# Attention and a token and channel mixer on one core: far tiles in one transfer, the ring of weight tiles on SyncE, and sums of weights stored at once

## The chip, the cores and the metric

The kernel runs on one core of a Trainium2 chip. The metric is the device time of one execution in microseconds. A core has TensorE (PE in the profile; PEld are its weight loads), VectorE (DVE), ScalarE (ACT), GpSimd (POOL) and SyncE (SP). DMAs are issued here by SyncE and by ScalarE, in the order of their programs, and run on 16 DMA engines.

## What is computed

The reference, cut to what matters (batch 8, 8 heads, 576 positions, head size 64, all float32):

```python
# attention inside chunks of 64 positions
scores = (q_c @ k_c^T) / sqrt(64)            # (8, 8, 9, 64, 64)
attn = softmax(scores)                       # with + 1e-9 in the denominator
x = (attn @ v_c) as (8, 576, 512)            # heads side by side
# mixer
h  = relu(x^T @ w_tok1) @ w_tok2             # over positions: 576 -> 256 -> 576
u  = x + h^T
h2 = relu(u @ w_ch1) @ w_ch2                 # over channels: 512 -> 1536 -> 512
return u + h2
```

## The kernel before, in words

Every float32 operand of the mixer is split into two float32r parts, high and low, and a product is three matmuls (high by high, low by high, high by low). The 4608 columns (batch by position) are handled in stages.

*First batch* (to about 210 us): the weights are converted, split and kept in SBUF while the first 576 columns go through both mixers.

*Single blocks* (to about 350 us): two blocks of 512 columns. Each runs 12 steps of a first channel matmul `ch1` and 12 of a second, `ch2`; a counter `now` (0 to 47) counts them, one step being 12 matmuls of 512 columns. Beside them run *bursts* of attention for the later batches (`attention`, called from a list of steps), and the preparation of Strassen-Winograd products: `sum_step` adds and splits blocks of the weights, 24 halves in all, each into one buffer of tag `sparts` (`SUM_BUFS` = 3); those of `c1` are made on GpSimd, those of `c2` on VectorE, at the steps in `SUMS`. The third step of a half puts its two blocks on the list `dumps`, where blocks of the raw weights (`dump_raw`, three at each step of `RAW_AT`) stand too; `dump(DUMPS)` stores two of the list to DRAM in each step, in order, from SyncE (L872).

*Pairs* (from about 350 us): three pairs of blocks run as products of that scheme, 84 per pair: 42 of the first channel weights (`product`, L1064) and 42 of the second (L1244), six matmuls each. Product k reads half of a *ring* tile, 512 KB, which comes back from DRAM. Ring tiles (`RING` = 5) are asked for by `load_product`, on ScalarE's queue, in ScalarE's order (`in_turn` holds an instruction behind the last one of its engine): the load of tile t stands at product 2t - 7, and its buffer is free after product 2t - 9. The function `unit(s)` is called behind product s and runs bursts (nine in pair 0, four in pair 1, every 7 or 8 products), loads and the mixing of the next pair. At s = 40 and 44 the token weights are read back (`load_tokens`), needed from s = 66.

*A burst* k scores tile k, and multiplies the probabilities of tile k - 2 with v in one PSUM tile. VectorE subtracts the maximum, ScalarE takes the exponential, `far_out` transposes 32 by 32 blocks on VectorE (L387) and SyncE writes them to DRAM (L392); `far_in` reads them back transposed, in four DMAs, one for each 32 partitions (L398): into `pf` for the probabilities (issued one step, or in the pairs four products, behind the burst; copied to `pt` ahead of burst k + 2), and into `xt` for the output x, which also goes to `xh` and `xl` for the token mixer.

The order of SyncE's instructions is that of the program in all stages. TensorE's is written out by hand from the end of the first batch; the others follow a planner's estimate of time, except what stands in `in_turn`. The framework gives the DMAs of both queues one of eight completion semaphores in turn; an issue waits on its own queue until the transfer that had that semaphore before has landed.

Of the kernel before, what the change touches and what calls it, by code (L numbers as in the profile page):

```python
# [18 lines left out]
P = 128  # L19
# [27 lines left out]
KH = 2 * P  # L47
RING = 5
LAG = 2
# [50 lines left out]
def attention_mixer_kernel(ctx, tc, qk_in, vo_in, v_in, w1_in, w2_in, wc1_in, wc2_in, out):  # L100
# [192 lines left out]

    def load_qk(i):
        qk = pool.tile([P, 2, NHP, P], F32, tag="qk" if i > 4 else "qk0", name="qk", bufs=3 if i > 4 else 5)
        nc.sync.dma_start(out=qk.rearrange("p a b c -> p (a b c)"), in_=qk_in[i])
        tiles[i] = {"qk": qk}

    def load_v(i):
# [7 lines left out]
        nc.sync.dma_start(out=v.rearrange("p a b c -> p (a b c)"), in_=src)  # L307
        tiles[i]["v"] = v

    def attn_load(i):  # L310
        load_qk(i)
        load_v(i)
# [550 lines left out]
    wide = ctx.enter_context(tc.tile_pool(name="wide", bufs=1, space=bass.MemoryType.DRAM))  # L863
    stored, tokens, dumps = {}, {}, []

    def dump(n):

        for key, src in dumps[:n]:
            two, one = divmod(products.index(key), 2)
            if two not in stored:  # L870
                stored[two] = wide.tile([P, 2, 2, KH], F32, tag=f"w_{two}", name="w")
            nc.sync.dma_start(out=stored[two][:, one], in_=src if src.dtype == F32 else src.bitcast(F32))  # L872
        del dumps[:n]
# [7 lines left out]
    def store_token():  # L881

        keys = [p[0] for p in plan[:token]] + ["half"]
        if len(tokens) < len(keys):
            key = keys[len(tokens)]
            src = half_all[0] if key == "half" else tops[key, "parts"]
            d = wide.tile([P, 2, src.shape[-1]], F32, tag="wt_" + "_".join(map(str, key)), name="wt")
            nc.sync.dma_start(out=d, in_=src.bitcast(F32))
            tokens[key] = d
# [32 lines left out]
    def attention(k):  # L922
# [3 lines left out]
        attn_both(i, j)  # L926
        if k + 2 < len(order):
            attn_load(order[k + 2])
        load_waiting(1)
        if i is not None:  # L930
            attn_p(i)
            tiles[i]["far"] = far_out(tiles[i]["pr"])
            attn_z(i)
        ready = len(waiting)
        if j is not None:
# [60 lines left out]
    def sum_step(kind, p, step):  # L996
# [40 lines left out]
        else:  # L1037
            for k, n in enumerate(SUM_KEYS[kind][half]):
                dumps.append(((kind, p, n), of[half][:, k]))

    def dump_raw(p):

        for n, f, h in ((0, 2 * p, 0), (3, 2 * p + 1, 1), (5, 2 * p + 1, 0)):
            dumps.append((("c2", p, n), weights["c2", f][:, :, h * KH:(h + 1) * KH]))

    ring = []
    def load_product(upto):
        while len(ring) < min(upto, PAIRS * len(products)):
            w = pool.tile([P, 2, 2, KH], F32, tag="ring", name="ring", bufs=RING)
            with in_turn():  # L1050
                nc.scalar.dma_start(out=w, in_=stored[len(ring) % len(products) // 2])
            ring.extend(w[:, one] for one in range(2))

    def product(i, u, width):

        load_product(i + 2 * RING - 2)
        if i % 3:
# [4 lines left out]
        for j in range(2):  # L1062
            for q, (wi, ui) in enumerate(THREE):
                nc.tensor.matmul(  # L1064
                    ps, lhsT=w[:, wi, j * P:(j + 1) * P].bitcast(F32R), rhs=u[ui][j],
                    start=j == 0 and q == 0, stop=j == 1 and q == 2,
                )
        return ps

    def load_tokens(kinds):  # L1070

        for key, d in tokens.items():
            if (key if key == "half" else key[0]) not in kinds:
                continue
            w = pool.tile(list(d.shape), F32, tag="again_" + "_".join(map(str, key)), name="again", bufs=1)
# [60 lines left out]
    def pair(n, rs):  # L1136
# [10 lines left out]
        def unit(s):  # L1147
# [31 lines left out]
        for p in range(NFC // 2):  # L1179
# [50 lines left out]
        for s, (step, p) in enumerate(steps):  # L1230
            while len(ready) <= min(s + SPLIT_AHEAD, len(steps) - 1):
                ready.append(operand(*steps[len(ready)]))
            load_product(first + PRODUCTS + s + 2 * RING - 2)
            if s == 0:
# [7 lines left out]
            for m in range(2):  # L1242
                for q, (wi, gi) in enumerate(THREE):
                    nc.tensor.matmul(  # L1244
                        accs[m], lhsT=w[:, wi, m * P:(m + 1) * P].bitcast(F32R), rhs=ready[s][gi],
                        start=p == 0 and q == 0 and step in (0, 1, 5, 6),
# [24 lines left out]
    for k in range(SINGLE):  # L1271
        at, width = BLOCKS[k]
        accs, pend = [], None
        for f in range(NFC):
            for half in range(2):
# [19 lines left out]
                if RING_AT <= now < RING_AT + RING - 1:  # L1295
                    load_product(2 * (now - RING_AT + 1))
                if now in TOKENS_TO:
# [71 lines left out]
```

## Time and profile before

| | us |
|---|---|
| median of 3 runs | 792.76 (789.87 to 801.0) |
| the profiled execution | 803.92 |
| its span, first to last instruction | 802.1 |
| busy: PE, PEld, DVE, ACT, POOL | 749.9, 621.9, 541.2, 350.0, 275.9 |
| mean granted TensorE clock | 0.972 |

The rows below come from that one execution. Its time is its span and what lies around it. PE's busy time holds all of its matmuls; what another engine idles costs nothing by itself, unless PE waits for it. A clock of 1.00 is 2.4 GHz, 0.50 is 1.2 GHz.

### The profile page before, as it was taken

Reading aid. Unit: us, or ns where it says so; the run is one execution under the profiler, and the core shown is the slowest. Engines: PE = TensorE matmul, PEld = TensorE weight load, DVE = VectorE, ACT = ScalarE, POOL = GpSimd, SP = SyncE. Lnnn points to the kernel's source line nnn. Section 1 sums busy time; section 2 is a strip of 40 time slices with the busy share of each in tenths; the row PEclk is TensorE's granted clock in tenths of the full one; section 3 lists DMA queues with packets and bytes.
Section 4 is the critical chain, followed back from the end, with each engine's and each line's share of the span. In section 5 each row is a group of like instructions: output and inputs, shape, how many; then the busy total and the mean of one; then the engine's idle time right before and its main releaser. Section 6 shows DMA issues by size and latency. Waiting matters only on the chain. (4 is left out here: it accounts for less than half of the span.)

```text
span 802.1 us, 14800 instructions
## 1 busy us (share of the span) xinstructions
PE 749.9 (93%) x5622; PEld 621.9 (78%) x5622; DVE 541.2 (67%) x861; ACT 350.0 (44%) x649; POOL 275.9 (34%) x223
## 2 busy tenths in 40 slices
PE   6899999999899977989999877999998999999998
PEld 4589998878677855778777665898786888888886
DVE  5899955667456546668675756598644887743795
ACT  6899833343232233233445433344434434443442
POOL 0000020625325351402443246204544851445460
PEclk9999999999997987999999998999999999999999
DMA  9955357578874786764999988635878754566664
GB/s 350 407 183 192 112 167 243 185 248 260 290 234 149 251 261 223 242 231 152 307 308 287 333 290 234 183 131 155 279 266 292 232 159 166 181 207 200 226 214 147
DMA packets 101622, 183.99 MB, mean 229 GB/s; under 512 B 11504, under 2 KB 50160, under 8 KB 101552
## 3 DMA queue, kind: packets, MB, share of 16 engines
q1 hardware_dynamic: 83408, 116.99, 43.8%
q10 hardware_dynamic: 18144, 66.07, 25.4%
q8 instruction: 44, 0.72, 0.4%
q14 instruction: 26, 0.21, 0.1%
HBM read 131.37 MB, written 50.72 MB: 227 GB/s over the span
## 5 line engine op out<-in xcount | busy, mean ns | idle before, releaser
L1064 PE MATMUL ps_p<-bh,ring 128*128 128x512 f32 (+1 forms) x504 | 154.9, 388 | 2.5 <-DMA ring<-w 2.4
L1244 PE MATMUL acc<-ph,ring 128*128 128x512 f32 (+1 forms) x432 | 135.1, 394 | 5.0 <-ACT ph L1210 4.4
L1211 DVE TENSOR_TENSOR pl<-cs,ph 128x512 fp32r<-128x512 f32 (+1 forms) x126 | 112.9, 932 | 30.8 <-ACT ph L1210 27.9
L1064 PEld LDWEIGHTS ps_p<-bh,ring 128*128 128x128 f32 x504 | 93.6, 188 | 21.5 <-DVE cs L1133 2.3
L1210 ACT CAST ph<-cs 128x512 fp32r<-128x512 f32 (+1 forms) x126 | 72.0, 608 | 70.0 <-PE acc L1244 21.0
L476 POOL TENSOR_TENSOR xl<-x,xh 128x512 fp32r<-128x512 f32 x28 | 40.5, 1455 | 179.3 <-ACT xh L475 150.1
L1244 PEld LDWEIGHTS acc<-ph,ring 128*128 128x128 f32 x432 | 82.5, 192 | 21.8 <-ACT ph L1210 5.2
L714 PE MATMUL acc<-gh,kept_c 128*128 128x288 f32 (+1 forms) x384 | 96.8, 355 | 0.9 <-ACT gh L683 0.9
L1064 PE MATMUL ps_p<-bl,ring 128*128 128x512 f32 (+1 forms) x252 | 97.2, 386 | 0.0
L1244 PE MATMUL acc<-pl,ring 128*128 128x512 f32 (+1 forms) x216 | 85.9, 398 | 4.0 <-DVE pl L1211 3.7
L714 PEld LDWEIGHTS acc<-gh,kept_c 128*128 128x128 f32 x384 | 65.8, 194 | 9.9 <-ACT gh L683 1.6
L1176 ACT ACTIVATE cs<-cs 128x512 f32<-128x512 f32 (+1 forms) x72 | 42.6, 619 | 70.6 <-DVE cs L1133 59.2
L672 PE MATMUL ps_c<-uh,kept_c 128*128 128x512 f32 x192 | 61.5, 402 | 5.5 <-DVE rl L591 5.0
L1133 POOL TENSOR_TENSOR cs<-cs 128x512 f32<-128x512 f32 (+1 forms) x36 | 46.2, 1304 | 42.5 <-ACT cs L1176 41.2
L714 PE MATMUL acc<-gl,kept_c 128*128 128x288 f32 (+1 forms) x192 | 59.6, 349 | 0.0
L1064 PEld LDWEIGHTS ps_p<-bl,ring 128*128 128x128 f32 x252 | 47.3, 188 | 9.1
L1244 PEld LDWEIGHTS acc<-pl,ring 128*128 128x128 f32 x216 | 41.4, 192 | 15.8 <-DVE pl L1211 8.1
L344 ACT ACTIVATE pr<-pr 128x512 f32<-128x512 f32 x36 | 22.7, 630 | 60.6 <-DVE pr L340 38.8
L672 PEld LDWEIGHTS ps_c<-uh,kept_c 128*128 128x128 f32 x192 | 36.5, 193 | 13.9 <-DVE rl L591 5.4
L672 PE MATMUL ps_c<-both,kept_c 128*128 128x288 f32 x288 | 43.7, 299 | 0.1
L1204 POOL TENSOR_TENSOR cs<-cs 128x512 f32<-128x512 f32 (+1 forms) x18 | 28.0, 1584 | 38.9 <-DVE pl L1211 38.9
L672 PEld LDWEIGHTS ps_c<-both,kept_c 128*128 128x128 f32 x288 | 39.5, 188 | 1.1 <-DVE gl L684 0.5
(143 smaller groups left out, 1429.7 us busy)
## 6 DMA issues: line engine op xcount, KB each, us to landing
ring<-w ACTq DMA_DIRECT2D x126, 512.0 KB, 4.4
qk<-in_qk SPq DMA_DIRECT2D x36, 512.0 KB, 5.4
far<-blocks SPq DMA_DIRECT2D x63, 256.0 KB, 4.0
raw_c<-in_wc SPq DMA_DIRECT2D x24, 512.0 KB, 9.6
w<-sparts SPq DMA_DIRECT2D x48, 256.0 KB, 2.9
w<-kept_c SPq DMA_DIRECT2D x36, 256.0 KB, 3.6
pf<-far SPq DMA_DIRECT2D x124, 64.0 KB, 2.9
v<-in_v SPq DMA_DIRECT2D x27, 256.0 KB, 5.4
```

Of the source, the lines that this page charges most:

```text
L344: nc.scalar.activation(out=pr, in_=pr, func=AF.Exp, scale=1.0 / float(D) ** 0.5)
L476: nc.gpsimd.tensor_tensor(out=xl, in0=t["own"], in1=xh.bitcast(F32), op=ALU.subtract)
L672: nc.tensor.matmul(ps[:, :width], lhsT=weights["c1", f][:, wi, k // 2, k % 2 * P:(k % 2 + 1) * P], rhs=u[ui][k], start=(k == 0 and q == 0) ...
L714: nc.tensor.matmul(accs[e], lhsT=weights["c2", f][:, wi, e * P:(e + 1) * P], rhs=g[gi], start=(f == 0 and q == 0), stop=(f == NFC - 1 and ...
L1064: nc.tensor.matmul(ps, lhsT=w[:, wi, j * P:(j + 1) * P].bitcast(F32R), rhs=u[ui][j], start=j == 0 and q == 0, stop=j == 1 and q == 2,)
L1133: (engine or nc.vector).tensor_tensor(out=c, in0=a, in1=b, op=op)
L1176: nc.scalar.activation(out=c, in_=c, func=AF.Relu)
L1204: nc.gpsimd.tensor_tensor(out=s1[p], in0=g11[p], in1=s1[p], op=ALU.subtract)
L1210: nc.scalar.copy(out=gh, in_=src)
L1211: (nc.gpsimd if LOW_ON_POOL[step] else nc.vector).tensor_tensor(out=gl, in0=src, in1=gh.bitcast(F32), op=ALU.subtract)
L1244: nc.tensor.matmul(accs[m], lhsT=w[:, wi, m * P:(m + 1) * P].bitcast(F32R), rhs=ready[s][gi], start=p == 0 and q == 0 and step in (0, 1, 5 ...
```

## The change

`far_out` transposes with groups interleaved, so that one DMA of 128 partitions reads a tile back. Ring tiles are asked for by SyncE, eight of them, by `load_ring`: the load of tile t stands at product 2t - 12 and its buffer is free after product 2t - 15. Sums of weights are stored in the step that ends them, with four buffers. Token weights come back one every three products from s = 41. Loads of qk and v stand behind a burst's far write. GpSimd makes `u4` ahead of `g22`, and ScalarE's ReLU of `g22` stands behind that of `g12`. `RESIDENT` is empty and `bulk[0]` stays SyncE's queue, so the code for other cases changes nothing.

```diff
-RING = 5
+RING = 8
-SUM_BUFS = 3
+SUM_BUFS = 4
+AGAIN_AT = 41
+RESIDENT = ()
...
         nc.vector.transpose(
             out=blocks.rearrange("p (g n c) -> p n g c", g=4, c=BK),
-            in_=src.rearrange("p (n g c) -> p n g c", g=4, c=BK),
+            in_=src.rearrange("p (n c g) -> p n g c", g=4, c=BK),
         )
-        far = dram.tile([P, DM], F32, tag=tag, name="far", bufs=4 if tag == "far" else 24)
-        nc.sync.dma_start(out=far, in_=blocks)
+        far = dram.tile([4, P, P], F32, tag=tag, name="far", bufs=4 if tag == "far" else 24)
+        nc.sync.dma_start(out=far.rearrange("i (c g) n -> (i c) (g n)", g=4), in_=blocks)
...
-        for g in range(4):
-            nc.sync.dma_start(
-                out=dst[g * BK:(g + 1) * BK].rearrange("p i n c -> p i (n c)"),
-                in_=far[rows, g * P:(g + 1) * P].rearrange("(i p) n -> p i n", p=BK),
-            )
+        nc.sync.dma_start(
+            out=dst.rearrange("p i n c -> p i (n c)"),
+            in_=far[rows.start // BK:rows.stop // BK].rearrange("i p n -> p i n"),
+        )
...
+    def keep(key, src, engine):
+
+        two, one = divmod(streamed.index(key), 2)
+        if two not in stored:
+            stored[two] = wide.tile([P, 2, 2, KH], F32, tag=f"w_{two}", name="w")
+        engine.dma_start(out=stored[two][:, one], in_=src if src.dtype == F32 else src.bitcast(F32))
...
         attn_both(i, j)
-        if k + 2 < len(order):
-            attn_load(order[k + 2])
         load_waiting(1)
         if i is not None:
             attn_p(i)
             tiles[i]["far"] = far_out(tiles[i]["pr"])
             attn_z(i)
+        if k + 2 < len(order):
+            with in_turn():
+                load_qk(order[k + 2], bulk[0])
+                load_v(order[k + 2], bulk[0])
...
             for k, n in enumerate(SUM_KEYS[kind][half]):
-                dumps.append(((kind, p, n), of[half][:, k]))
+                keep((kind, p, n), of[half][:, k], nc.sync)
...
-    def load_product(upto):
-        while len(ring) < min(upto, PAIRS * len(products)):
+    def load_ring(now, most=RING):
+
+        t = len(tiles_in)
+        while 2 * t < len(asked) and (t < most or most == RING):
+            if t >= RING and asked[2 * (t - RING) + 1] >= now - 2:
+                break
             w = pool.tile([P, 2, 2, KH], F32, tag="ring", name="ring", bufs=RING)
             with in_turn():
-                nc.scalar.dma_start(out=w, in_=stored[len(ring) % len(products) // 2])
-            ring.extend(w[:, one] for one in range(2))
+                nc.sync.dma_start(out=w, in_=stored[t % (len(streamed) // 2)])
+            for one in range(2):
+                ring[asked[2 * t + one]] = w[:, one]
+            tiles_in.append(w)
+            t += 1
...
-        load_product(i + 2 * RING - 2)
+        load_ring(i)
...
-            if s == PRODUCTS - 2:
-                load_tokens(("t1", "half"))
+            if s >= AGAIN_AT and (s - AGAIN_AT) % 3 == 0:
+                load_tokens((s - AGAIN_AT) // 3)
             if s == PRODUCTS + 2:
-                load_tokens(("t2",))
                 open_x(k + 2, k + 3)
...
             p5 = snap(product(j + 3, own[3], width), width)
+            u4 = plus(p5, u2, width, "sum", nc.gpsimd)
             unit(i + 3)
             u3 = plus(product(j + 4, own[4], width), u2, width, "sum")
-            u4 = plus(p5, u2, width, "sum", nc.gpsimd)
-            g22.append(relu(plus(p5, u3, width, "cs", nc.gpsimd)))
+            g22.append(plus(p5, u3, width, "cs", nc.gpsimd))
             unit(i + 4)
             g12.append(relu(plus(product(j + 5, own[5], width), u3, width, "cs")))
+            relu(g22[p])
```

## Rows read from the trace of the kernel before

**Rows 1.** Busy us (and count) of each engine by stretch, granted clock, DMA share, GB/s.

```profile
40.00:210.00 170.00, 166.76 (x1536) 147.46 (x1536) 121.24 (x223) 92.90 (x183) 40.16 (x36) 0.99 0.63 205
...
210.00:350.00 140.00, 120.75 (x1016) 97.20 (x1014) 82.66 (x137) 42.91 (x83) 51.16 (x45) 0.89 0.73 237
...
400.00:500.00 100.00, 86.12 (x731) 66.04 (x724) 67.96 (x105) 41.08 (x79) 46.32 (x34) 0.95 0.90 292
...
550.00:690.00 140.00, 136.26 (x790) 112.47 (x789) 99.04 (x132) 58.26 (x106) 63.12 (x44) 1.00 0.65 217
```

**Rows 2.** The same view of two stretches of 512-column matmuls.

```profile
492.40:497.40 5.00, 5.00 (x12) 3.91 (x13) 3.70 (x6) 2.38 (x5) 2.71 (x2) 0.50 0.93 259
...
620.00:630.00 10.00, 10.00 (x45) 8.29 (x45) 7.88 (x11) 3.99 (x8) 4.62 (x3) 1.00 0.60 221
```

**Rows 3.** Timeline, TensorE: start, us, instruction, [idle before it, who ended it].

```profile
215.41 0.73 PE L573 MATMUL ps_t<-xh,kept_t 128*128 128x512 f32 x2 [3.09 <-ACT xh L475]
...
298.60 1.22 PE L672 MATMUL ps_c<-uh,kept_c 128*128 128x512 f32 x2 [4.97 <-DVE rl L591]
...
342.57 0.73 PE L573 MATMUL ps_t<-xh,kept_t 128*128 128x512 f32 x2 [2.31 <-ACT xh L475]
```

**Rows 4.** Timeline, VectorE, ScalarE (ACT) and its queue (ACTq), ahead of those waits.

```profile
210.08 0.43 DVE L1029 TENSOR_TENSOR sparts<-wsum 128x256 f32<-128x256 f32 x1 [6.00 <-DMA w<-sparts]
...
296.61 0.62 ACT L1033 CAST sparts<-sparts 128x512 fp32r<-128x512 f32 x1 [6.70 <-POOL sparts L1029]
...
340.45 0.34 ACTq L1051 DMA_DIRECT2D ring<-w  x1
...
340.90 0.63 ACT L344 ACTIVATE pr<-pr 128x512 f32<-128x512 f32 x1 [5.54 <-DMA w<-sparts]
```

**Rows 5.** Waits, whole span: us in total, times, longest us.

```profile
POOL sparts L1029 <- DMA w<-sparts: 20.8, 5, 7.6
...
DVE sparts L1029 <- DMA w<-sparts: 18.6, 5, 6.0
```

**Rows 6.** Timeline, SyncE's queue, ScalarE and TensorE in the first pair.

```profile
446.81 5.99 SPq L398 DMA_DIRECT2D pf<-far  x4
...
469.53 0.33 ACTq L1051 DMA_DIRECT2D ring<-w  x1
...
469.90 0.62 ACT L1210 CAST ph<-cs 128x512 fp32r<-128x512 f32 x1 [7.43 <-DMA again<-wt]
...
470.57 1.22 PE L1244 MATMUL acc<-ph,ring 128*128 128x512 f32 x2 [2.64 <-ACT ph L1210]
```

**Rows 7.** DMA issues by tile: ns min/median/max, first and last start; landing of ring and pf.

```profile
L1051 ACTq DMA_DIRECT2D ring<-w x126: 326/326/514, 340.5 to 784.1; - x126
...
DMA to landing us min/median/max: 3.1/4.4/10.8
...
L398 SPq DMA_DIRECT2D pf<-far x124: 302/430/1392, 55.7 to 574.0; - x124
...
DMA to landing us min/median/max: 1.8/2.9/10.9
...
L398 SPq DMA_DIRECT2D xt<-far x156: 302/430/1768, 70.9 to 662.6; - x156
```

**Rows 8.** Waits of SyncE's queue, whole span: us in total, times, longest us.

```profile
SPq L1221 <- DVE o L1219: 127.8, 22, 14.8
...
SPq L392 <- DVE blocks L387: 96.8, 34, 11.3
```

**Rows 9.** Groups by line and shape (VectorE whole span, ScalarE 0 to 130 us): busy us, mean ns.

```profile
L1211 DVE TENSOR_TENSOR pl<-cs,ph 128x512 fp32r<-128x512 f32 x84 | 77.1, 951 | 23.9 <-ACT ph L1210 23.4
...
L387 DVE STREAM_TRANSPOSE blocks<-x 128x512 f32<-128x512 f32 x32 | 22.4, 701 | 0.1
...
L197 ACT ACTIVATE wtop<-raw_c 128x512 f32<-128x512 f32 x24 | 16.7, 694 | 0.1
...
L262 ACT CAST kept_c<-wtop 128x512 fp32r<-128x512 f32 x12 | 7.7, 638 | 1.4 <-DVE wtop L217 1.4
```

More of the change, by code (lines that the diff above doesn't have):

```diff
@@ L292, in block_x, with load_qk, load_v @@
         return xts[k]
-    def load_qk(i):
+    def load_qk(i, engine=nc.sync):
         qk = pool.tile([P, 2, NHP, P], F32, tag="qk" if i > 4 else "qk0", name="qk", bufs=3 if i > 4 else 5)
-        nc.sync.dma_start(out=qk.rearrange("p a b c -> p (a b c)"), in_=qk_in[i])
+        engine.dma_start(out=qk.rearrange("p a b c -> p (a b c)"), in_=qk_in[i])
         tiles[i] = {"qk": qk}
-    def load_v(i):
+    def load_v(i, engine=nc.sync):
         if i < NTILE:
@@ L306, in load_v @@
             src = v_in[i - NTILE]
-        nc.sync.dma_start(out=v.rearrange("p a b c -> p (a b c)"), in_=src)
+        engine.dma_start(out=v.rearrange("p a b c -> p (a b c)"), in_=src)
         tiles[i]["v"] = v
@@ L863, in attention_mixer_kernel @@
     wide = ctx.enter_context(tc.tile_pool(name="wide", bufs=1, space=bass.MemoryType.DRAM))
-    stored, tokens, dumps = {}, {}, []
+    streamed = [key for key in products if key[0] == "c1" or key[2] not in (3, 5) or key[1] not in RESIDENT]
+    stored, tokens, dumps, bulk = {}, {}, [], [nc.sync]
+    def keep(key, src, engine):
[3 more added lines that the diff above has]
+        engine.dma_start(out=stored[two][:, one], in_=src if src.dtype == F32 else src.bitcast(F32))
     def dump(n):
         for key, src in dumps[:n]:
[L869 to L872, printed above, removed]
+            with in_turn() if bulk[0] is nc.scalar else ExitStack():
+                keep(key, src, bulk[0])
         del dumps[:n]
@@ L887, in store_token @@
             d = wide.tile([P, 2, src.shape[-1]], F32, tag="wt_" + "_".join(map(str, key)), name="wt")
-            nc.sync.dma_start(out=d, in_=src.bitcast(F32))
+            with in_turn():
+                bulk[0].dma_start(out=d, in_=src.bitcast(F32))
             tokens[key] = d
@@ L933, in attention @@
             attn_z(i)
+        if k + 2 < len(order):
+            with in_turn():
+                load_qk(order[k + 2], bulk[0])
+                load_v(order[k + 2], bulk[0])
         ready = len(waiting)
@@ L1038, in sum_step, with f32r @@
             for k, n in enumerate(SUM_KEYS[kind][half]):
-                dumps.append(((kind, p, n), of[half][:, k]))
+                keep((kind, p, n), of[half][:, k], nc.sync)
     def dump_raw(p):
         for n, f, h in ((0, 2 * p, 0), (3, 2 * p + 1, 1), (5, 2 * p + 1, 0)):
-            dumps.append((("c2", p, n), weights["c2", f][:, :, h * KH:(h + 1) * KH]))
-    ring = []
-    def load_product(upto):
-        while len(ring) < min(upto, PAIRS * len(products)):
+            if ("c2", p, n) in streamed:
+                dumps.append((("c2", p, n), weights["c2", f][:, :, h * KH:(h + 1) * KH]))
+    ring, tiles_in = {}, []
+    for i in range(PAIRS * len(products)):
+        key = products[i % len(products)]
+        if key not in streamed:
+            h = (5, 3).index(key[2])
+            ring[i] = weights["c2", 2 * key[1] + 1][:, :, h * KH:(h + 1) * KH]
+    asked = [i for i in range(PAIRS * len(products)) if i not in ring]
+    def load_ring(now, most=RING):
[3 more added lines that the diff above has]
+                break
             w = pool.tile([P, 2, 2, KH], F32, tag="ring", name="ring", bufs=RING)
             with in_turn():
-                nc.scalar.dma_start(out=w, in_=stored[len(ring) % len(products) // 2])
-            ring.extend(w[:, one] for one in range(2))
+                nc.sync.dma_start(out=w, in_=stored[t % (len(streamed) // 2)])
[3 more added lines that the diff above has]
+            t += 1
+    def f32r(w):
+        return w if w.dtype == F32R else w.bitcast(F32R)
     def product(i, u, width):
-        load_product(i + 2 * RING - 2)
+        load_ring(i)
         if i % 3:
@@ L1064, in product @@
                 nc.tensor.matmul(
-                    ps, lhsT=w[:, wi, j * P:(j + 1) * P].bitcast(F32R), rhs=u[ui][j],
+                    ps, lhsT=f32r(w[:, wi, j * P:(j + 1) * P]), rhs=u[ui][j],
                     start=j == 0 and q == 0, stop=j == 1 and q == 2,
@@ L1068, in product, with load_tokens @@
         return ps
[L1070 to L1074, printed above, removed]
+    def load_tokens(n):
+        for key in sorted(tokens, key=lambda k: (k != "half", k[0] == "t2"))[n:n + 1]:
+            d = tokens[key]
             w = pool.tile(list(d.shape), F32, tag="again_" + "_".join(map(str, key)), name="again", bufs=1)
@@ L1232, in pair @@
                 ready.append(operand(*steps[len(ready)]))
-            load_product(first + PRODUCTS + s + 2 * RING - 2)
+            load_ring(first + PRODUCTS + s)
             if s == 0:
@@ L1244, in pair @@
                     nc.tensor.matmul(
-                        accs[m], lhsT=w[:, wi, m * P:(m + 1) * P].bitcast(F32R), rhs=ready[s][gi],
+                        accs[m], lhsT=f32r(w[:, wi, m * P:(m + 1) * P]), rhs=ready[s][gi],
                         start=p == 0 and q == 0 and step in (0, 1, 5, 6),
@@ L1295, in attention_mixer_kernel @@
                 if RING_AT <= now < RING_AT + RING - 1:
-                    load_product(2 * (now - RING_AT + 1))
+                    load_ring(0, now - RING_AT + 1)
                 if now in TOKENS_TO:
```

## The prediction

> **What bounds the kernel now.** I read the stretches first. TensorE is the bound nearly everywhere, so only its idle time and its time at the lower clock can be won; from 40 to 210 us it idles 3.24 of 170 us [rows 1]. Three stretches lose more. From 210 to 350 us (the single blocks, while sums of weights are made and stored) it is busy 120.75 of 140 us, idle 19.25. From 400 to 500 us (the first pair, with nine bursts of attention) it idles 13.88 of 100, and from 550 to 690 us (the second pair, four bursts) 3.74 of 140. The granted clock adds to that: a mean of 0.89 over 140 us is (1 - 0.89) / 0.5 x 140 = 30.8 us at 1.2 GHz, and 0.95 over 100 us is 10. What this costs is in the counts of matmuls of 512 columns: 45 in 10 us at a clock of 1.00, 12 in 5 us at 0.50 [rows 2], so a microsecond at 1.2 GHz loses 1 - 2.4 / 4.5 = 0.47 us. The stretches with the lower clock are those with the idle time, so I let it go in the same share. To be won at most: 19.25 + 14.5, 13.88 + 4.7 and 3.74, together 56 us.
>
> Next, who causes it. The timeline of TensorE names ScalarE or VectorE, as in the waits of 3.09, 4.97 and 2.31 us [rows 3], but these were held themselves [rows 4]. VectorE stood 6.00 us to 210.08 us before its first sum of weights, because the buffer it wanted was still being stored; the x that TensorE needed stood behind that sum in VectorE's order. ScalarE stood 6.70 us to 296.61 us for GpSimd, which was waiting for a store of the same kind. In the list of waits these stores hold VectorE 18.6 us in five waits and GpSimd 20.8 us in five, up to 7.6 us [rows 5]. The wait at 342.57 us has another cause: ScalarE reached a DMA issue of the ring, which could start only at 340.45 us when a store of SyncE had landed, and the exponential and xh behind it came 5.54 us late [rows 4].
>
> That second cause rules the first pair: at 469.53 us a ring issue on ScalarE got free when a token weight had landed, the cast behind it was 7.43 us late and TensorE waited 2.64 us for it [rows 6]. The eight completion semaphores go round over all DMAs of both queues, so an issue waits for the transfer eight issues earlier, whoever asked for it; four issues for one tile use up half of them. Four reads of one far tile held SyncE 5.99 us there instead of some 1.7 [rows 6, 7].
>
> **The change, part by part.** *Sums leave first, four buffers.* A sum stores in the step that finishes it, not behind raw weights at two stores a step. Take step 14: its second sum takes the buffer whose stores were queued at 13 behind three of step 12, so the last leaves at 15, a whole step (12 matmuls, 2.7 us by [rows 2]) after VectorE wants it. With four buffers and no queue, every buffer of the list was handed to SyncE three steps (8 us) or more before it is wanted again. The 39.4 us of waits of [rows 5] go. Late next are the ordinary chain from x to xh and xl, and the far round trip. New: SyncE waits at the store for the split of the sum, one step earlier in the order; what queues behind it are reads with 10 us of slack, so nothing is charged.
>
> *Ring on SyncE, eight tiles.* ScalarE loses 126 issues of 0.326 us, 41 us, and every hold like those of [rows 4, 6]. SyncE gains 41 us but loses three of four far reads: 124 + 156 issues become 70, and 210 x 0.43 = 90 us go [rows 7]. A ring issue on SyncE now waits for the product three before it, and out stores, far writes, qk and v queue behind it; a product is six matmuls, 1.33 us [rows 2], so SyncE runs at most 4 us ahead of TensorE. In return a ring tile stands in line behind SyncE's own waits: 22 for out (longest 14.8 us) and 34 for a transposed tile (longest 11.3) [rows 8]. A tile is asked for when the product 15 before its first use has ended, so 14 products or 18.7 us remain (eight products, 10.7 us, before); landing takes 4.4 us in the middle case, at most 10.8 [rows 7]. SyncE may then be 14 us late in the middle case without TensorE seeing it, as long as its longest wait for out. Price: 0 to 10 us; I take 3, since the middle landing and all but the longest waits fit.
>
> *One transfer per tile.* Besides the issues, a pf or xt tile should land about three issues, 1.3 us, earlier. The bytes and the 512-byte pieces stay. The transpose now reads with a step of four floats instead of one. No row of VectorE shows that; its transpose takes 701 ns [rows 9]. ScalarE reading every second float takes 694 ns against 638 for plain ones; VectorE's slowest common operation of this size takes 951 [rows 9]. So each of 63 transposes costs 0 to 0.25 us, 0 to 16 us of VectorE's time; I take the near row's 0.06, 4 us, of which 1 on the path, since VectorE is busy 82.66 of 140 us and 67.96 of 100 [rows 1].
> The Trainium skill ("SBUF — State Buffer", Door 1: The DMA port swizzle) says that an access to a new 16-byte line pays a penalty, and that four floats is as far as one can step for free. This step lies just on that edge: by the first half the transposes slow down (rival 3), by the second they cost nothing (the sum without its 1 us); no row here decides.
>
> *Smaller edits.* The token weights come back one in three products from product 41 (first needed at 66) instead of in two bunches: nothing to pay. Loads of qk and v behind the far write of a burst are needed two bursts later: nothing. The sum u4 first on GpSimd, and the ReLU of g22 behind that of g12, take a wait for GpSimd out of ScalarE's order: 0 to 1 us won, taken as 0.
>
> **The sum.** From 210 to 350 us I take three quarters of 33.7: 25 us; the rest is the wait of xl on GpSimd and the far round trip. From 400 to 500 us I take 10 of 18.6: the DMA engines are busy 0.90 there at 292 GB/s [rows 1], which makes 324 at a full share, and the same bytes need 90 us at that rate. From 550 to 690 us, 2.5 of 3.74. Won 37.5, paid 3 + 1: net 33.5. The profiled execution took 803.92 us (its span and 1.8 us around it), so 770.4; it stands 1.4% over the median of the runs, 792.76, and the same share of that gives 760 us, 4.1% faster.
>
> **Rivals.**
> 1. *The DMA engines become the bound of the first pair.* For: busy 0.90, and 237 GB/s at 0.73 from 210 to 350 us points to the same 325 at most [rows 1]. Against: a share of 0.90 with TensorE idle leaves a tenth, and eight tiles ahead smooth the load. Then only 25 + 2.5 - 4 are won: 780, or 770 by the median. Chance 0.18.
> 2. *One queue for all; slower.* Far reads now stand behind ring tiles of 512 KB. In the pairs pf is asked for four products behind a burst and needed eight products (10.7 us) later. It decides when a ring tile's worst landing lies ahead of it: 10.8 + 2.9 = 13.7 us [rows 7], 3 us too late, in 13 bursts 39 us; the lower clock cost 14.5 us beside 19.25 of idle time before, in the same ratio 29 more. With the 25 us won in the single blocks: 847, or 835 by the median. Against: the middle landing of 4.4 + 2.9 = 7.3 us fits. Chance 0.06.
> The Trainium skill ("DMA: Bandwidth & Descriptors", Queues, rings and completion order) speaks for this rival: each DMA engine takes turns between the queues with work, and within one queue goes in order, so with a second queue for the ring a small read passes and with one it doesn't.
> 3. *The transposes slow down* to the upper end or beyond: 16 us more on VectorE, half of it on the path of bursts, 8: 778, or 768. Chance 0.06.
> 4. *Room.* Three ring tiles and one sum buffer take 16 KB more of each partition, and waits for space taken by other tiles replace those won in the pairs: 780 to 795, or 769 to 784. Chance 0.05.
> 5. *The stores leave no earlier*, since SyncE reaches them late, held by far writes: a third of the 25 us remains, and the ring's gain: 787, or 776. Chance 0.05.
>
> **How the numbers follow.** My forecast has 0.60: 760 us. Its own ends are 50 us won (744) and 18 (775). The range takes rivals 1, 3 and 5 in and most of 4: 743 to 785. About 2% (16 us) is what a measurement of this kernel tells from no change. Faster by more than that (under 777): the forecast, three quarters of rival 1 and parts of 3 to 5, 0.80. Slower: rival 2, 0.05. The rest, 0.15, is the same.
>
> **What would show it.** Right: no wait of sparts on its store; no DMA issue on ScalarE and no cast of ph behind a landing; TensorE idle 5 to 8 us from 210 us to the end of the single blocks and the clock at 1.00 there; transposes near 0.70 us. Wrong: waits of TensorE on the ring in most bursts (SyncE too late), a DMA share over 0.95 through the first pair, ps_sv waiting for pt, or stalls of the same length under other names.

## The result and the profile after

The changed kernel took 766.98 us (median of 4 runs, 766.26 to 767.17) beside 796.88 us for the kernel before (789.87 to 801.98): a ratio of 0.9651, 95% interval 0.9564 to 0.9739. It is 3.5% faster, 28 us by the ratio and 30 by the medians. (A difference of ratios is turned into us below by 796 us, the kernel before.) The profiled execution took 766.87 us, 37 us less than the one before (803.92). The ratios leave out executions of the kernel before that are over 1.5% above its fastest, and its profiled execution lies 7 to 9 us above the mean of those that are kept, so lengths of stages set against it can make a gain too large by as much.

Of the kernel after, part 1 of the page (busy us of each engine, share of the span, instructions), and the stretches, with the columns of [rows 1]:

```profile
PE 734.3 (96%) x5622; PEld 614.5 (80%) x5622; DVE 573.1 (75%) x861; ACT 350.5 (46%) x649; POOL 277.8 (36%) x223
```

```profile
40.00:210.00 170.00, 165.14 (x1535) 145.80 (x1535) 134.72 (x233) 95.66 (x188) 43.01 (x39) 1.00 0.62 211
210.00:350.00 140.00, 133.43 (x1154) 111.92 (x1153) 107.98 (x162) 50.07 (x93) 49.90 (x44) 0.98 0.75 255
400.00:500.00 100.00, 92.91 (x644) 76.32 (x643) 79.95 (x107) 44.32 (x84) 40.66 (x28) 0.95 0.78 277
550.00:690.00 140.00, 139.96 (x671) 117.86 (x671) 95.15 (x123) 58.88 (x106) 65.45 (x47) 1.00 0.67 233
```

Against [rows 1]: from 210 to 350 us TensorE idles 6.6 us instead of 19.25, at a clock of 0.98 instead of 0.89. From 400 to 500 us it idles 7.1 instead of 13.88, at the same clock. From 550 to 690 us nothing is left. The DMA engines are busy 0.78 of the stretch from 400 to 500 us instead of 0.90 and move nearly the same bytes, 277 GB/s against 292. VectorE is busier: 573.1 us in all, 541.2 before.

Since the work of a fixed window shifts, I also cut each trace at four events in TensorE's timeline: the first product of a single block (`ps_c` from `uh`), and the first product of each pair. Lengths in us (kernels are named in the sections below):

```
                         head  singles  pair 1  pair 2  pair 3
before                  151.1    222.5   173.0   141.8   113.7
after                   149.7    200.6   163.4   137.7   113.7
sums alone              149.8    204.6   171.8   143.5   113.4
ring on SyncE alone     149.9    216.4   183.0   139.1   113.6
one transfer alone      149.0    208.7   164.8   141.2   113.9
sums and one transfer   150.4    205.3   163.6   140.3   113.9
four transfers again    150.0    207.7   167.6   137.7   113.8
plain transposes        151.4    195.1   158.0   137.6   113.7
half the partitions     151.7    207.0   163.4   137.9   113.6
ring on ScalarE         150.6    201.6   163.3   140.4   113.6
ring of five            150.5    198.5   187.0   138.0   113.8
turned P                149.9    198.0   157.8   137.6   113.9
```

Of the 37 us between the two profiled executions, 21.9 lie in the single blocks, 9.6 in the first pair, 4.1 in the second and 1.4 in the head.

The waits of the kernel after (us in total, times, longest us) show which holds went. Those on a store of a sum, and ScalarE's waits on DMAs other than its first loads:

```profile
ACT pt L416 <- DMA pf<-far: 14.3, 5, 4.1
...
ACT xr L503 <- DMA xc<-x: 5.1, 3, 2.4
...
POOL sparts L1039 <- DMA w<-sparts: 1.7, 2, 1.3
...
ACT bh L1136 <- DMA ring<-w: 0.6, 1, 0.6
```

VectorE and GpSimd stood 39.4 us for such stores [rows 5]; 1.7 us remain. No cast of `ph` stands behind a landing any more, as it did for 7.43 us [rows 6]. The long waits of TensorE that remain in the first pair end with VectorE. From 210 to 350 us, the waits of TensorE that remain are these:

```profile
PE ps_sv L366 <- issue: 2.6, 1, 2.6
PE ps_sv L378 <- ACT pt L416: 1.9, 1, 1.9
PE ps_c L673 <- DVE gl L685: 1.4, 1, 1.4
PE ps_t L645 <- DVE gl L685: 0.7, 1, 0.7
```

In the first pair, the timeline of the kernel after (columns as in [rows 3]) has TensorE's second-longest wait and VectorE ahead of it:

```profile
456.11 1.11 DVE L389 STREAM_TRANSPOSE blocks<-pr 128x512 f32<-128x512 f32 x1
457.14 0.65 DVE L352 TENSOR_REDUCE zs<-pr 128x8 f32<-128x512 f32 x1
457.70 1.09 DVE L389 STREAM_TRANSPOSE blocks<-x 128x512 f32<-128x512 f32 x1
458.73 5.00 DVE L1238 TENSOR_TENSOR pl<-cs,ph 128x512 fp32r<-128x512 f32 x3
...
460.42 0.80 PE L1271 MATMUL acc<-pl,ring 128*128 128x512 f32 x1 [2.51 <-DVE pl L1238]
```

VectorE has no idle time from 456 to 463 us: two transposes of 1.1 us and a reduction stand ahead of the split that TensorE wants. The groups by line and shape (busy us, mean ns, idle before) give the transposes of the whole span, and the views of `ring` and `pf` give their landings:

```profile
L389 DVE STREAM_TRANSPOSE blocks<-x 128x512 f32<-128x512 f32 x32 | 35.0, 1094 | 0.1
L389 DVE STREAM_TRANSPOSE blocks<-pr 128x512 f32<-128x512 f32 x31 | 34.2, 1103 | 5.8 <-ACT pr L346 4.7
```

```profile
L1073 SPq DMA_DIRECT2D ring<-w x126: 319/390/2124, 319.1 to 734.7; - x126
...
DMA to landing us min/median/max: 3.1/6.0/10.1
```

```profile
L399 SPq DMA_DIRECT2D pf<-far x31: 370/536/1150, 56.3 to 540.6; - x31
...
DMA to landing us min/median/max: 2.7/5.8/9.0
```

A transpose takes 0.39 us more than the 701 ns of [rows 9]: 25 us of VectorE for 63 of them.

### The profile page after: what moved, and what is told of

It is laid out like the page before. It is cut to its first block, busy times and chain, and to the rows that moved or that the text cites. A ratio compares the mean times of both kernels' runs of the same rounds, so it can differ in the third digit from the quotient of the medians.

```text
span 765.1 us, 14619 instructions
## 1 busy us (share of the span) xinstructions
PE 734.3 (96%) x5622; PEld 614.5 (80%) x5622; DVE 573.1 (75%) x861; ACT 350.5 (46%) x649; POOL 277.8 (36%) x223
## 5 line engine op out<-in xcount | busy, mean ns | idle before, releaser
L1092 PE MATMUL ps_p<-bh,ring 128*128 128x512 f32 (+1 forms) x504 | 156.9, 393 | 3.0 <-DVE sum L1160 2.9
L1271 PE MATMUL acc<-ph,ring 128*128 128x512 f32 (+1 forms) x432 | 132.9, 389 | 0.0
L1238 DVE TENSOR_TENSOR pl<-cs,ph 128x512 fp32r<-128x512 f32 (+1 forms) x126 | 118.1, 978 | 13.5 <-ACT ph L1237 11.9
L1092 PEld LDWEIGHTS ps_p<-bh,ring 128*128 128x128 f32 x504 | 95.2, 190 | 21.9 <-DVE sum L1160 3.4
L715 PE MATMUL acc<-gh,kept_c 128*128 128x288 f32 (+1 forms) x384 | 95.2, 350 | 1.1 <-ACT gh L684 1.0
L1237 ACT CAST ph<-cs 128x512 fp32r<-128x512 f32 (+1 forms) x126 | 71.4, 608 | 43.1 <-POOL cs L1233 15.3
L673 PE MATMUL ps_c<-uh,kept_c 128*128 128x512 f32 x192 | 59.9, 393 | 2.1 <-DVE gl L685 2.1
L1160 POOL TENSOR_TENSOR cs<-cs 128x512 f32<-128x512 f32 (+1 forms) x36 | 46.8, 1321 | 39.1 <-ACT cs L1202 32.2
L685 DVE SCALAR_TENSOR_TENSOR gl<-ps_c,gh 128x512 fp32r<-128x512 f32 (+1 forms) x36 | 21.7, 604 | 26.3 <-ACT gh L684 26.3
```

What stands on the lines that cost most here:

```text
L673: nc.tensor.matmul(ps[:, :width], lhsT=weights["c1", f][:, wi, k // 2, k % 2 * P:(k % 2 + 1) * P], rhs=u[ui][k], start=(k == 0 and q == 0) ...
L685: nc.vector.scalar_tensor_tensor(out=gl, in0=ps[:, :width], scalar=0.0, in1=gh.bitcast(F32), op0=ALU.max, op1=ALU.subtract)
L715: nc.tensor.matmul(accs[e], lhsT=weights["c2", f][:, wi, e * P:(e + 1) * P], rhs=g[gi], start=(f == 0 and q == 0), stop=(f == NFC - 1 and ...
L1092: nc.tensor.matmul(ps, lhsT=f32r(w[:, wi, j * P:(j + 1) * P]), rhs=u[ui][j], start=j == 0 and q == 0, stop=j == 1 and q == 2,)
L1160: (engine or nc.vector).tensor_tensor(out=c, in0=a, in1=b, op=op)
L1237: nc.scalar.copy(out=gh, in_=src)
```

## The experiments

My theory after the result: the sums and the ring's move brought the gain, as forecast, and the transposes took about half of 25 us back. The rivals: the gain of the pairs belongs to the one transfer per tile, not to the ring's queue; the transposes cost nothing, since VectorE is not the bound. Each kernel was timed beside the kernel before on the same chip, and every ratio is to that.

### Sums alone

Before, with sums stored in the step that ends them:

```diff
-SUM_BUFS = 3
+SUM_BUFS = 4
...
-                dumps.append(((kind, p, n), of[half][:, k]))
+                nc.sync.dma_start(out=stored[two][:, one], in_=src)
```

> The kernel before with the sums alone changed: stored in their own step, four buffers. If VectorE and GpSimd standing for these stores is what costs the single blocks their time, the stretch from the end of the first batch to the first product (222 us before, 201 us in the changed kernel) is shortened by 12 to 18 us, not by all 22, since a ring issue on ScalarE caused one of its waits and the four-issue reads stay; the pairs keep their idle time; 777 to 785 us. If the four issues per tile were the cause, the stores wait behind them as before and the time stays within 5 us of before.

Measured: 785.08 us beside 797.96, ratio 0.9852 (0.9815 to 0.989), 12 us by the ratio, the low end of what the theory gave. The row for 210 to 350 us of this kernel, columns as above:

```profile
210.00:350.00 140.00, 130.33 (x1136) 108.90 (x1135) 93.45 (x154) 49.39 (x94) 50.23 (x44) 0.95 0.75 244
```

TensorE's idle time falls from 19.25 to 9.7 us and the clock rises from 0.89 to 0.95. The single blocks are 17.9 us shorter, the pairs together are not. The first cause stands: VectorE waits for no store of a sum any more. GpSimd still stands 20.5 us for one, to 301.42 us. Of TensorE's idle time here most is now one wait for the far round trip, which four reads of a tile still make:

```profile
295.58 1.13 PE L376 MATMUL ps_sv<-v,pt 64*64 64x64 f32 x32 [8.44 <-ACT pt L415]
```

### Ring on SyncE alone

```diff
-                nc.scalar.dma_start(out=w, in_=stored[len(ring) % len(products) // 2])
+                nc.sync.dma_start(out=w, in_=stored[len(ring) % len(products) // 2])
```

The ring keeps five tiles.

> The kernel before with one word changed: ring loads issued by SyncE, still five tiles (eight do not fit into SBUF beside the old order). If ScalarE held by its DMA issues is the cause in the pairs, no cast of ph waits for a landing any more and the first two pairs win 5 to 12 us; five tiles leave 10.7 us ahead, so some waits for the ring itself come instead. 783 to 792 us. If the issues of far reads on SyncE are the cause, the ring stands behind them and TensorE waits for the ring in most bursts: the time of before or up to 15 us more.

Measured: 801.31 us, ratio 1.0069 (1.0035 to 1.0102): 0.7% slower. The first theory's gain did not come, and the time is in the second's range. ScalarE's casts of `ph` stand 1.3 us behind a landing, 23.2 in the kernel before. That line of the waits, then TensorE's waits for the ring and the longest of them in its timeline:

```profile
ACT ph L1210 <- DMA out<-o: 1.3, 1, 1.3
...
PE acc L1244 <- DMA ring<-w: 13.4, 3, 6.6
...
PE ps_m L1244 <- DMA ring<-w: 5.2, 2, 2.7
...
PE ps_p L1064 <- DMA ring<-w: 3.2, 2, 2.0
```

```profile
478.49 1.19 PE L1244 MATMUL acc<-ph,ring 128*128 128x512 f32 x2 [6.61 <-DMA ring<-w]
```

The move alone takes the holds from ScalarE and makes TensorE wait 21.8 us for the ring in seven waits: with five tiles, ring tiles stand behind SyncE's other work and come late. The first pair grows by 10 us; the second is 2.7 us shorter.

### One transfer alone

Before, with the new `far_out` and `far_in` of the diff and nothing else.

> The kernel before with the far tiles alone changed: one transfer back, the transpose with a step of four. My theory: less is issued, but VectorE pays 0.40 us for each of 63 transposes, 25 us, and the stores of sums and ring issues hold as before: from 5 us less to 5 us more than before. The rival, that fewer issues free the eight completion semaphores and with them everything else: 775 us or less, with the waits of ScalarE for landings gone.

Measured: 780.95 us, ratio 0.9812 (0.9778 to 0.9846), 15 us better by the ratio where I expected at most 5, though its transposes take 1.1 us. The first pair is 8.2 us shorter with the ring still on ScalarE, and the single blocks 13.8. Its row for 400 to 500 us:

```profile
400.00:500.00 100.00, 93.25 (x696) 74.56 (x697) 79.52 (x102) 42.46 (x80) 45.38 (x31) 0.97 0.81 284
```

The DMA engines are busy 0.81 instead of 0.90 for almost the same rate, 284 GB/s. So this edit, which I had booked at a loss of 1 us, is by itself the largest part of the change in the first pair. The rival has something in it too: ScalarE's waits of `ph`, `cs` and `pr` on transfers sum to 11.3 us, against 43.1 in the kernel before. The cause could be the smaller number of transfers or their shape.

### Four transfers again

After, with the old `far_out` and `far_in`, plain transposes included.

> The changed kernel with far tiles as before: four transfers back, the plain transpose. If the gain is in the sums and in the queue of the ring, this keeps it, and VectorE gets 25 us back, while SyncE pays 90 us of issues: 762 to 772 us beside 767. If the one transfer carries the gain: 780 us and more, with TensorE waiting for ring tiles that stand behind far reads.

Measured: 773.54 us, ratio 0.9727 (0.9677 to 0.9776), 6.6 us over the kernel after, although its transposes take 0.70 us. Its first-pair stretch, and TensorE's longest wait:

```profile
400.00:500.00 100.00, 89.39 (x668) 71.00 (x667) 69.65 (x98) 40.08 (x77) 44.78 (x31) 0.93 0.89 280
```

```profile
295.71 1.14 PE L378 MATMUL ps_sv<-v,pt 64*64 64x64 f32 x32 [9.27 <-ACT pt L417]
```

The DMA engines are back at 0.89 for 280 GB/s, and TensorE waits 9.27 us for `pt`, which ScalarE copies from a tile of `pf` that has not landed.

### Plain transposes, one transfer

```diff
-            in_=src.rearrange("p (n c g) -> p n g c", g=4, c=BK),
+            in_=src.rearrange("p (n g c) -> p n g c", g=4, c=BK),
```

> The changed kernel with the plain transpose (groups of 32 neighbouring floats) ahead of the one transfer: the far tiles then come back with their partitions in another order, so the values of the output are not the reference's, while every transfer keeps its size and place. It measures the step of four by itself. Expected 0.70 us for a transpose in place of 1.09, 25 us off VectorE. If VectorE is the late engine in what is left of the waits (pl behind two transposes at 454 and 458 us, gl), 3 to 7 us are won: 760 to 764 us. If VectorE's time is hidden everywhere, the time stays within 1 us of 767.

Measured: 756.2 us (753.59 to 757.59) beside 795.9, ratio 0.9499 (0.9458 to 0.954). The groups and the first pair:

```profile
L389 DVE STREAM_TRANSPOSE blocks<-x 128x512 f32<-128x512 f32 x32 | 22.4, 701 | 0.1
L389 DVE STREAM_TRANSPOSE blocks<-pr 128x512 f32<-128x512 f32 x31 | 22.0, 708 | 6.1 <-ACT pr L346 5.3
```

```profile
400.00:500.00 100.00, 94.28 (x688) 78.08 (x687) 81.73 (x116) 43.67 (x83) 40.84 (x29) 1.00 0.79 276
```

The step of four floats costs 766.98 - 756.2 = 10.8 us of the time (12 by the ratios), nearly half of the 25 us on VectorE. This kernel measures the step alone; its output is in another order than the reference's. TensorE idles 5.7 us in this stretch at a granted clock of 1.00, 7.1 at 0.95 in the kernel after. The rival by which the transposes hide falls.

### Half the partitions

After, with a step of two floats in the transpose and two transfers of 64 partitions per tile. The far tile is then written in pieces of 1 KB instead of 2 KB:

```diff
-            in_=src.rearrange("p (n c g) -> p n g c", g=4, c=BK),
+            in_=src.rearrange("p (n a c b) -> p n a b c", a=2, b=2, c=BK),
...
+        for a in range(2):
+            nc.sync.dma_start(
+                out=dst[a * 2 * BK:(a + 1) * 2 * BK].rearrange("p i n c -> p i (n c)"),
...
```

> The changed kernel with far tiles in two transfers of 64 partitions, so that the transpose reads with a step of two floats. If the cost of the step comes from touching a new 16-byte line with each float, two floats a line are enough and a transpose takes 0.70 us; if it comes from any step but one, it stays near 1.09. SyncE issues 70 more reads, 30 us of its queue, which should be hidden, and a tile takes two of the eight semaphores. With 0.70 us: 761 to 766 us; with 1.09: 767 to 771.

Measured: 776.05 us, ratio 0.9763 (0.9715 to 0.9811). Its groups, the first pair and TensorE's longest wait:

```profile
L389 DVE STREAM_TRANSPOSE blocks<-x 128x512 f32<-128x512 f32 x32 | 22.4, 700 | 0.5 <-DMA far<-blocks 0.4
```

```profile
400.00:500.00 100.00, 92.59 (x698) 74.27 (x697) 72.85 (x103) 41.59 (x80) 45.06 (x32) 0.97 0.94 296
```

```profile
292.62 1.13 PE L378 MATMUL ps_sv<-v,pt 64*64 64x64 f32 x32 [5.38 <-ACT pt L420]
```

A step of two floats is free, 700 ns. But the kernel is 20 us slower than the one above, with the same transposes: the DMA engines are busy 0.94, and `pt` is late again.

### Two transfers of all partitions

The kernel with plain transposes, its read cut into two by rows of tokens, each to 128 partitions:

```diff
+        for i in range(0, n, 2):
+            nc.sync.dma_start(
+                out=dst[:, i:min(i + 2, n)].rearrange("p i n c -> p i (n c)"),
...
```

> After with plain transposes and two transfers per tile that both go to all 128 partitions, cut by rows of 32 tokens; what comes out is in another order of features. Theory (it is the number of transfers in SyncE's round of eight that costs, whatever their shape): near the kernel with two transfers of 64 partitions, 770 to 778 us. Rival (it was the shape, half of the partitions and pieces of 1 KB): near the kernel with plain transposes and one transfer, 755 to 761 us.

Measured: 753.46 us, ratio 0.9462 (0.9405 to 0.9519). Its first pair:

```profile
400.00:500.00 100.00, 94.96 (x684) 78.55 (x683) 83.18 (x114) 42.83 (x82) 41.16 (x28) 0.98 0.77 272
```

My theory here, that the number of transfers in the round of eight semaphores is what costs, falls: twice as many cost nothing. What the slow kernels share is that a read-back reaches only part of the partitions. Rate over busy share in this stretch gives the bytes that the engines move when busy: 324 GB/s before [rows 1], 315 with four of 32 partitions, 315 with two of 64; 355 after, 349 and 353 with one and with two of 128.

The window holds somewhat different work in each kernel, but the packets of the whole first pair, 44 to 45 MB in all of them, say the same. Their time, over 16 engines, is 125 to 128 us in the nine kernels with reads to 128 partitions and 135 to 141 us in the five with reads to 32 or 64. The far reads' own packets of 512 bytes take 28 to 29 ns against 32 to 37, and those of 4096 bytes, the ring's among them, 177 to 190 against 195 to 205: the transfers beside them are slower too. The pieces of 1 KB in the kernel with two of 64 are hardly the cause: they take 48 ns each, as long for each byte as its packets of 2 KB (96 ns), and the kernels with four of 32 write pieces of 2 KB.

### Ring on ScalarE, and a ring of five

After, each with one line changed:

```diff
-                nc.sync.dma_start(out=w, in_=stored[t % (len(streamed) // 2)])
+                nc.scalar.dma_start(out=w, in_=stored[t % (len(streamed) // 2)])
```

```diff
-RING = 8
+RING = 5
```

> The changed kernel with the ring's loads issued by ScalarE again, eight tiles at the same products. If ScalarE's holds came from the count of transfers in the round of eight semaphores, which one transfer per tile has already cut from 719 to 509, the queue matters little now: 765 to 770 us, and casts of ph wait little for landings. If the queue itself was the cause, the holds are back and the first pair loses 8 to 12 us: 775 to 779.

> The changed kernel with five ring tiles. They leave 10.7 us between a buffer's end and the next use, less landing (6.0 us in the middle) 5 us for SyncE's own waits, of which many are longer. If eight tiles are what makes SyncE's queue bearable, TensorE waits for the ring in most bursts and 10 to 25 us are lost: 777 to 792. If SyncE reaches the loads in time anyhow, up to 3 us.

Measured: 770.6 us with the ring on ScalarE, ratio 0.9676 (0.9627 to 0.9724), and 792.03 us with five tiles on SyncE, ratio 0.9949 (0.9922 to 0.9975). ScalarE's waits in the former, the longest four of those that hold its ring issues:

```profile
ACT ph L1237 <- DMA xt<-far: 7.0, 2, 5.3
...
ACT xh L476 <- DMA xt<-far: 6.4, 1, 6.4
ACT cs L1202 <- DMA ring<-w: 5.5, 2, 2.7
...
ACT snap L1155 <- DMA ring<-w: 4.9, 1, 4.9
```

TensorE's waits in the latter:

```profile
PE acc L1271 <- DMA ring<-w: 11.3, 4, 5.3
PE ps_p L1092 <- DMA ring<-w: 9.5, 4, 3.2
```

With the ring on ScalarE the holds are back, 6.4 us at most, and still the time rises by only 3.6 us, within the interval. In the first pair the queue is worth nothing (163.3 and 163.4 us). In the second it seems to be worth the 3 us: that pair takes 137.6 to 139.1 us in the table's kernels with the ring on SyncE, 140.3 to 143.5 in those with it on ScalarE. The room is worth more: on SyncE, five tiles cost 25 us, nearly all of it in the first pair (187.0 us against 163.4).

### Sums and one transfer

Before with these two parts; the ring stays on ScalarE with five tiles.

> Before with two parts of the change: sums of weights stored at once with four buffers, and one transfer per tile with its transpose; the ring stays at five tiles on ScalarE. Theory (the parts add, the sums alone gave 12 us, the one transfer alone 15 us, and with one transfer the ring's queue and room are worth some 3 us more): 767 to 772 us. Rival (without the ring on SyncE with eight tiles the parts take each other's gain away): 778 to 785 us.

Measured: 773.05 us (770.61 to 775.22) beside 798.83, ratio 0.9694 (0.9633 to 0.9756). The parts add, nearly: by the ratios 12 and 15 us alone, 24 together. What remains of the change, the ring and the smaller edits, brings 3 us by the ratios and 6 by the medians; the intervals overlap, and the first pair is as long without it (163.6 and 163.4 us). The single blocks are where the two parts share a gain: 17.9 and 13.8 us alone, 17.2 together.

### Turned P, and turned P and x: a faster kernel

The spread order can be made without a step in the transpose. ScalarE writes the exponentials of P in turned order, into a second buffer of the same tag, the sum over keys reads them so, and the rows of v are reordered to match:

```diff
-        nc.scalar.activation(out=pr, in_=pr, func=AF.Exp, scale=1.0 / float(D) ** 0.5)
+        to = pr
+        if i > 4:
+            to = t["pr"] = pool.tile([P, DM], F32, tag="pr", name="pe")
+            to = to.rearrange("p (h a c) -> p a h c", a=2, c=16)
+            pr = pr.rearrange("p (a h c) -> p a h c", a=2, c=16)
+        nc.scalar.activation(out=to, in_=pr, func=AF.Exp, scale=1.0 / float(D) ** 0.5)
...
-            t = pool.tile([P, N], F32, tag="ts", name="ts", bufs=4)[:, :width]
+            t = pool.tile([P, N], F32, tag="ts", name="ts", bufs=3)[:, :width]
```

The second kernel does the same for x: ScalarE writes r with a step of four floats into an extra tile, and GpSimd copies the first batch's x.

> After, but the exponentials of P (31 of the 63 turned tiles) are written by ScalarE in such an order that VectorE can transpose them with a step of one float and the spread token order comes out right; v's rows are reordered to match, and three buffers instead of four for the sums of b make the room. The kernel computes the whole reference. Theory (the step of four floats costs VectorE 0.39 us a tile, and all 63 together 11 us of the time): about half of that comes back, 760 to 763 us, with 31 transposes at 0.70 us. Rival (ScalarE pays for the turned write what VectorE saves, exp above 1 us): 766 us, as after.

> The same for x as well: r is written in turned order by ScalarE, the first batch's x is copied in turned order by GpSimd, the weights of the channel mix are reordered to match; the ring has seven tiles instead of eight and the sums of b two buffers, for room. The kernel computes the whole reference. Theory: all 63 transposes at 0.70 us, 754 to 760 us, less what the seventh ring tile costs (five instead of eight cost 25 us, so up to 8 us for one): 755 to 764. Rival (the extra copies on ScalarE and GpSimd and the smaller ring take it back): 766 or more.

Measured: turned P 759.04 us (758.71 to 759.63) beside 798.83, ratio 0.953 (0.9481 to 0.9578); both turned 762.98 us, ratio 0.9575 (0.9521 to 0.963). Groups of the first kernel, then of the second, and in the second's timeline one wait of TensorE:

```profile
L398 DVE STREAM_TRANSPOSE blocks<-x 128x512 f32<-128x512 f32 x32 | 35.0, 1093 | 0.1
L398 DVE STREAM_TRANSPOSE blocks<-pe 128x512 f32<-128x512 f32 x31 | 21.9, 708 | 5.8 <-ACT pe L351 5.0
L351 ACT ACTIVATE pe<-pr 128x512 f32<-128x512 f32 x31 | 19.6, 632 | 55.8 <-DVE pr L342 55.8
```

```profile
L607 ACT ACTIVATE rg<-ps_t 128x512 f32<-128x512 f32 x14 | 15.1, 1082 | 27.4 <-PE ps_t L586 27.4
...
L471 POOL COPY xp<-x 128x512 f32<-128x512 f32 x5 | 6.4, 1288 | 27.9 <-DVE x L465 27.9
```

```profile
450.56 0.70 PE L1286 MATMUL acc<-ph,ring 128*128 128x512 f32 x2 [2.48 <-DMA ring<-w]
```

The exponentials cost the same in turned order (632 ns; 630 in the kernel after), where neighbouring pieces of 16 floats stay whole, and 31 transposes are back at 0.71 us. By the medians it is 8 us faster than the change (759.04 and 766.98), by the ratios 10; its runs and those of the kernel after do not overlap, though the two were not timed on one chip. Turning x as well gains nothing, 4 us are lost. Two things that come with it show in the trace: ScalarE's write with a step of four floats takes 1.08 us, and the ring of seven tiles that the room allows lets TensorE wait 2.48 us. No run tells them apart.

## Why the prediction was right, and where not

The forecast of 760 us was 0.9% low, and the kernel is faster as forecast, 3.5% where I gave 4.1%. By stretches the sum held: 25, 10 and 2.5 us won and 4 paid, against 21.9, 9.6 and 4.1 measured net, and 1.4 in the head; 33.5 against 37 between the profiled executions and 28 by the ratio. By its parts it held less well, and that the first pair came out right is luck: the ring's move, which was to win it, won nothing there once a far tile came back in one transfer, the one transfer won it, and the transposes cost ten times what they were booked at.

*Sums leave first.* Right. The 39.4 us of waits [rows 5] shrank to 1.7, and the part alone shortens the single blocks by 17.9 us. What I left for xl and the far trip, a quarter of 33.7, 8.4 us, is about what stayed: 6.6 us of idle time and a clock of 0.98, which is 5.6 us at 1.2 GHz, 2.6 lost. Of the two that I named only the far trip is among the waits that stayed, with 1.9 us; xl is not. And the sums alone left 9.7 us, 8.4 of them in one wait for the far trip, so the one transfer has a share in this gain.

*Ring on SyncE, eight tiles.* Here the prediction named the wrong owner of the gain. It let the second cause, ScalarE held at ring issues, rule the first pair. But the holds go and the kernel gets slower when only the queue moves, and with the ring back on ScalarE up to 6.4 us of hold costs 3.6 us in all, none of it in the first pair. Only beside four transfers does the ring with the smaller edits win something there: 171.8 us with the sums alone, 167.6 with four transfers again. The price that the step allowed, 0 to 10 us with eight tiles, is right: the list of waits after names none of TensorE on a ring tile, at a middle landing of 6.0 us (4.4 forecast, [rows 7]). The slack of 14 us that I worked out needs eight tiles; with five, TensorE waits 21.8 and 20.8 us for the ring. That is this step's price, not rival 2, whose late far reads did not come: a pf tile lands 5.8 us after its issue, at most 9.0, within the 10.7 that rival 2 allowed.

*One transfer per tile.* The term with the wrong sign. I counted issues and 1.3 us of landing, and held that the bytes and pieces stay. They do, but the DMA engines move them faster: 355 GB/s at a full share against 324. Alone it won 15 us by the ratio, slow transposes included. The earlier landing is not what did it: from the first issue to the last landing a pf tile takes 4.8 us in the middle case in the kernel before, 3.9 with this part alone and 5.8 in the kernel after. This is also where rival 1 was wrong: it took the 324 as a limit of the kernel, and it was one of its transfers to 32 partitions. The Trainium skill ("SBUF — State Buffer", The DMA setup-cost knee) asks for 128 partitions and for one large transfer; the runs agree with the first half (315 GB/s for parts, 349 to 355 for whole) and show nothing of the second, since two per tile were as fast as one.

*The transposes.* The mechanism was rival 3's, and only its size was off in the sum: 0.06 us each, 1 us on the path, became 0.39 and 10.8; the sign of transposes near 0.70 us did not come. The upper bound of 0.25 us, from VectorE's slowest common operation, did not hold either, since it came from another kind of operation. Rival 3's 8 us on the path was near, but its total was not, since the one transfer gave more than that back. The Trainium skill ("SBUF — State Buffer", Door 1: The DMA port swizzle) puts the free step at up to four floats; 0.70 us at two floats and 1.10 at four say that the fourth already pays, and the measurement decides. The half of the section by which each new line pays agrees.

*The scaling.* I took the profiled execution's excess of 1.4% over the median with me. After the change the profiled execution (766.87) stands at the median (766.98), so that excess did not last. The unscaled 770.4 is 3.4 us off, the scaled 760 7.0.

*Room and stores.* Rivals 4 and 5 did not come: the stretches won about what they should with eight tiles in place, and the sums leave in time.

What stays open: why a transfer to a part of the partitions slows the engines was not tried, only that kernels with such transfers are slower, at 32 and at 64. How much of the gain of one transfer comes through ScalarE's shorter holds, and whether these come from fewer transfers or from faster ones, is open too.

## What to carry over

Read the DMA rate over the busy share in the fullest stretch before taking it for a limit: if it differs between kernels with the same bytes, look at the shape of the transfers, as here. Cutting a tile by its free dimension keeps all partitions in each piece. When a change moves a reordering into another instruction, price that instruction by its own kind at that step, and look for an engine whose write can take the order in whole pieces. Transfers that move to a busier queue need more buffers: on SyncE's queue the ring with five tiles was 25 us slower than with eight.

## What the hardware showed that was not expected

- A 128x512 transpose on VectorE takes 0.70 us when it reads with a step of one or two floats, 1.09 to 1.10 with four. ScalarE's ReLU from TensorE's result takes 1.08 us when it writes with a step of four floats (0.60 without, to a tile of another type); its exponential in pieces of 16 floats takes 0.63 as in plain order.
- With transfers to 32 or 64 partitions the rate of the whole stretch was a tenth lower (315 against 349 to 355 GB/s at a full share), and 32 were no worse than 64. Packets of other transfers slowed with it: those of 4096 bytes took 195 to 205 ns in the first pair, 177 to 190 where all reads reached 128 partitions.
